# The first two units' output projection in seven products of halves, from combined weight blocks held in SBUF

## The chip, the cores and the metric

The kernel runs on one core of one Trainium2 chip. The metric is the device time of one execution in microseconds; a kernel's time is the median of its runs.

## What is computed

A retention block is followed by a gated feed-forward block. The inputs q, k and v have 8 batches, 8 heads, 576 positions and 64 channels. Cut to what matters:

```python
scores = (q @ k.transpose(0, 1, 3, 2)) / 8
Dmat = where(rel >= 0, gamma ** rel, 0)        # rel = pos[:, None] - pos[None, :], one gamma per head
attn = (scores * Dmat) @ v
x = attn.transpose(0, 2, 1, 3).reshape(4608, 512)
xn = x / sqrt(mean(x * x, axis=-1) + 1e-06) * rms_g
g = xn @ w_gate                                # 512 -> 1536
h = g / (1 + exp(-g)) * (xn @ w_val)
out = h @ w_out                                # 1536 -> 512
```

Activations are float32. The three weight matrices come in as 64-bit floats and are turned to float32 on the chip.

## The kernel before, in words

**Tiling.** The 4608 tokens are 12 units of 384. A unit's x is held transposed (`x_of`, 128 x 4 x 384: channels on partitions), and so is its hidden h (`h_of`, 128 x 12 x 384: hidden channels on partitions, 12 tiles of 128). The attention is done in 32 jobs, one for each batch and pair of heads. `slot(j)` (L397) computes the value products of job j-1, the scores and states of job j, weighs them on VectorE, and ends with the carried products of job j-1, whose results VectorE scales into x. `values` (L344) ends with a tiny GpSimd memset (`tick`, L359), and the first carried product (L370) waits for it: this keeps the order of rows in the array. `prepare` (L246) turns a job's q and k on VectorE (L251), `load_qk` and `load_kv` bring the next ones in on the SyncE queue. `following(j)` does the turn of job j+1 and the load of job j+2; q and k have one raw buffer each, so the load waits for the turn.

**Seven products.** From unit 2 on, both feed-forward stages multiply 2x2 blocks with seven products of half size in place of eight, after Winograd. The weights' combined blocks are called A11, A12, S1, A22, S2, S3 and S4 (S1 = A21 + A22, S2 = S1 - A11, S3 = A11 - A21, S4 = A12 - S2). For the up projections GpSimd makes them in place (`combine(m)`, L811 to L819: 12 operations of 128x512 for w_gate, m = 0, and 12 for w_val, m = 1). For the output, `across(u)` (L623) takes the halves of h: the blocks B11, B12 (first six tiles, left and right half of the tokens), B21 and B22. VectorE makes T1 = B12 - B11 and T3 = B22 - B12, later B11 + T3 and B21 - B11 (L649). `across` is a generator: the first step makes T1 and T3, and each later one issues one product of 12 matmuls of 128x192 (L637) in the order x, z, w, y, x, z, w; VectorE then adds the parts (L646), transposes the result in blocks of 32 (L659), and SyncE stores it in eight transfers of 24 KB (L669) for each of four quarters of the output. Three output tiles rotate, so the transpose of a fourth waits for the first one's stores.

**Blocks of w_out.** The seven blocks of w_out are kept in DRAM (`w_blocks`, stored by `keep`, L597), and `fetch` (L615) brings them one by one to four slots, in the room of w_out itself.

**The first two units.** Units 0 and 1 are computed while the weights still come in and are rounded, with plain products: `up_plain` (L552), then `down(u, s)` (L575), 12 matmuls of 128x512 (L578) into one bank for each 128 tokens, a copy on ScalarE (L583), one store. Unit 1's h lies in the upper half of w_val's room (blocks 8 to 13), and the upper half of w_gate's room serves the rounding as scratch until the last weights are done. After unit 1's last up product the order is: the turn of job 8 and the load of job 9, three blocks of w_out stored as they are, combine(0) on GpSimd, the three down parts of unit 1 with the norm of unit 2 between (squares on ScalarE added up by VectorE, L438; a mean by TensorE, L450; a power on GpSimd, L456; diagonals on VectorE, L463; a product that spreads them, L474; scaling and block sums on VectorE, L476 and L487), combine(1), slot 8 without a job before it, the down parts of unit 0, slot 9. The other four blocks of w_out are made by `combine_out` (L600), 24 VectorE operations of 128x256 (L608), one after each step of unit 2's up products, and are stored and fetched after them.

**What sets the order.** The order on each engine is the program's (`manual_schedule`): an instruction that waits holds all behind it on its engine. PSUM has five rotating banks, temporaries six rotating tiles; DMAs wait in turn for one of eight semaphores, so that an issue can wait for the landing of the eighth before it.

The stage as it stands, from `start`:

```python
        for u in (1, 0):
            for s in range(NS):
                down(u, s)
                if u == 1:
                    (norm_0, norm_1, norm_2)[s](2)
                    if s == 1:
                        diagonals(2)
            if u:
                combine(1)
                slot(8, rest=False)
                following(8)
        slot(9)
        following(9)
```

Of the kernel before, what the change touches and what calls it, by code (L numbers as in the profile page):

```python
# [41 lines left out]
def kernel(  # L42
# [44 lines left out]
    def bank(name):  # L87
        return banks.tile([P, 512], F32, tag="b", name=name)
# [483 lines left out]
                    nc.scalar.activation(out=h, in_=ps[:, :U], func=AF.Silu)  # L572
                yield

    def down(u, s):  # L575
        ps = bank(f"out_{u}_{s}")
        for f in range(NF):
            nc.tensor.matmul(  # L578
                ps[:, :DM], lhsT=h_of[u][:, f, s * P : s * P + P], rhs=w_out[:, f],
                start=(f == 0), stop=(f == NF - 1),  # L580
            )
        o = outs.tile([P, DM], F32, tag="o", name=f"o_{u}_{s}")
        nc.scalar.copy(out=o, in_=ps[:, :DM])  # L583
        nc.sync.dma_start(out=out[u * U + s * P : u * U + s * P + P, :], in_=o)


    ORDER = (A11, S1, S3, S2, A12, S4, A22)
    DH = DM // 2
    w_blocks = dram.tile([7, P, NH, DH], F32, name="w_blocks")
    w_slots = w_out.rearrange("p f d -> p (f d)").rearrange("p (s f d) -> p s f d", s=4, d=DH)  # L590
    n_fetched = 0

    def quarter(row, col):

        return w_out[:, col * NH : col * NH + NH, row * DH : row * DH + DH]

    def keep(blk, t):  # L597
        nc.sync.dma_start(out=w_blocks[blk], in_=t)

    def combine_out():  # L600

        a11, a12, a21, a22 = (quarter(r, c) for r in range(2) for c in range(2))
        for c in range(NH):
            for o, a, b, op in (
                (a22, a21, a22, ALU.add), (a21, a11, a21, ALU.subtract),
                (a11, a22, a11, ALU.subtract), (a12, a12, a11, ALU.subtract),
            ):
                nc.vector.tensor_tensor(out=o[:, c], in0=a[:, c], in1=b[:, c], op=op)  # L608
                yield
        for blk, t in ((S1, a22), (S3, a21), (S2, a11), (S4, a12)):  # L610
            keep(blk, t)
        for _ in range(4):
            fetch()

    def fetch():  # L615
        nonlocal n_fetched
        if n_fetched < 7 * (NU - 2):
            nc.sync.dma_start(
                out=w_slots[:, n_fetched % 4], in_=w_blocks[ORDER[n_fetched % 7]]
            )  # L620
            n_fetched += 1

    def across(u):  # L623


        h = h_of[u]
        b11, b12 = h[:, :NH, :HU], h[:, :NH, HU:]
        b21, b22 = h[:, NH:, :HU], h[:, NH:, HU:]
        t1 = ffn.tile([P, NH, HU], F32, tag="t1", name=f"t1_{u}")
        x_, y, z, w = (bank(f"{n}o_{u}") for n in "xyzw")  # L630
        s1, u2, u4 = (temp(f"{n}o_{u}") for n in ("m1", "u2", "u4"))

        def product(rhs, ps, start):
            k = 7 * (u - 2) + n_done
            for i in range(2):
                for c in range(NH):
                    nc.tensor.matmul(  # L637
                        ps[:, i * HU : i * HU + HU],
                        lhsT=w_slots[:, k % 4, c, i * P : i * P + P], rhs=rhs[:, c],
                        start=(start and i == c == 0), stop=False, skip_group_check=True,  # L640
                    )
            if n_done < 3:
                fetch()

        def add(o, a, ps):
            nc.vector.tensor_tensor(out=o, in0=a, in1=ps[:, :U], op=ALU.add)  # L646

        def block(o, a, b, op):
            nc.vector.tensor_tensor(out=o, in0=a, in1=b, op=op)  # L649

        def result(row, col, a, ps):
            r = ps[:, :U]
            if a is not None:
                r = temp(f"c{row}{col}_{u}")
                add(r, a, ps)
            o = outs.tile([P, DM], F32, tag="o", name=f"o_{u}_{row}_{col}")[:, :U]
            end = u == NU - 1
            if not end:
                nc.vector.transpose(out=o, in_=r)  # L659
            o_of = o.rearrange("p (d t r) -> p d t r", d=2, r=SQ)  # L660
            for d in range(2):
                if end:
                    half = slice(d * HU, d * HU + HU)
                    nc.vector.transpose(out=o[:, half], in_=r[:, half])
                for i in range(P // SQ):
                    c0 = row * DH + d * P + i * SQ
                    t0 = u * U + col * HU
                    queue = nc.scalar if end and i % 2 else nc.sync
                    queue.dma_start(  # L669
                        out=out[t0 : t0 + HU, c0 : c0 + SQ].rearrange("(t c) r -> c t r", c=SQ),  # L670
                        in_=o_of[i * SQ : i * SQ + SQ, d],
                    )

        n_done = 0
        block(t1, b12, b11, ALU.subtract)
        block(b12, b22, b12, ALU.subtract)
        yield
        product(b11, x_, True)
        nc.scalar.copy(out=s1, in_=x_[:, :U])
        block(b11, b12, b11, ALU.add)  # L680
        n_done += 1
        yield
        product(t1, z, True)
        n_done += 1
        yield
        product(b12, w, True)
        n_done += 1
        yield
        product(b11, y, True)
        add(u2, s1, y)  # L690
        add(u4, u2, z)
        result(1, 1, u4, w)
        n_done += 1
        yield
        product(b21, x_, False)
        result(0, 0, None, x_)
        block(b21, b21, b11, ALU.subtract)
        n_done += 1
        yield
        product(b22, z, False)  # L700
        result(0, 1, u2, z)
        n_done += 1
        yield
        product(b21, w, False)
        result(1, 0, u2, w)
        yield
# [147 lines left out]
    def start():  # L854
# [54 lines left out]
        gather(*squares.pop())  # L909
        load_qk(2 * NHP)  # L910
        load_kv(2 * NHP)
        for m, g in [(m, g) for g in range(NG) for m in range(2)]:
            for u in range(2):
                weights_to(4 * g + 2 * m + 1)
                for i, _ in enumerate(up_plain(u, m, g)):
                    if not (u or m or g):
                        if i == 0:
                            values(2 * NHP - 1)
                            carried(2 * NHP - 1)
                            gather(1, NHP - 1, square(1, NHP - 1))  # L920
                        elif i == 1:
                            norm_1(1)
                        elif i == 2:
                            diagonals(1)
                        elif i == 3:
                            norm_2(1)
                    weights(2)
                    act(1)
                    if i == 1:
                        weights_to(4 * g + 2 * m + 2)  # L930
        following(2 * NHP - 1)
        weights_to(len(chunks))
        for blk, row, col in ((A11, 0, 0), (A12, 0, 1), (A22, 1, 1)):
            keep(blk, quarter(row, col))
        combine(0)
        for u in (1, 0):
            for s in range(NS):
                down(u, s)
                if u == 1:
                    (norm_0, norm_1, norm_2)[s](2)  # L940
                    if s == 1:
                        diagonals(2)
            if u:
                combine(1)
                slot(8, rest=False)
                following(8)
        slot(9)
        following(9)

# [19 lines left out]
    with tc.manual_schedule():  # L969
        start()  # L970
        for u in range(2, NU):
            made = combine_out() if u == 2 else iter(())
            for i in range(2 * NG):
                for n, _ in enumerate(up(u, i % 2, i // 2)):
                    next(made, None)
                    if n == 2 and turns:
                        prepare_next(turns.pop())
                if u > 2 and i in (1, 3):
                    fetch()
                    fetch()  # L980
                if i == 2 * NG - 1:
                    rest = across(u)
                    next(rest)
                behind(u, i)
            for i, _ in enumerate(rest):
                if i == 0 and turns:
                    prepare_next(turns.pop())
                if i == 2:
                    behind(u, 6)
                    at, n = SLOTS[u % 3]  # L990
                    if 2 * NG - 1 in at:
                        load_next(u // 3 * 8 + n + len(at) - 1)
                elif i == 4:
                    behind(u, 7)
# [27 lines left out]
```

## Time and profile before

| what | value |
|---|---|
| median of three runs (lowest, highest) | 1153.94 us (1153.77, 1154.94) |
| the profiled execution's own time | 1159.48 us |
| its span in the profile | 1157.7 us |
| mean granted TensorE clock in it | 0.993 |
| busy in the span: TensorE, VectorE, ScalarE, GpSimd | 1133.4, 696.3, 246.1, 46.5 us |
| down products of unit 1, of unit 0 (L578) | 193.4 to 225.1, 226.9 to 258.0 us |
| combine(0), combine(1) on GpSimd (L819) | 184.07 to 200.76, 215.79 to 232.07 us |
| 24 operations of combine_out on VectorE (L608) | 416 ns each |
| a half-block subtraction of across (L649, 128x1152) | 1342 ns mean |
| store of one w_out block (768 KB), issue to landing | 6.0 us median |

Each row of the timeline has a start in microseconds from the span's start, a length, the engine, the line, the operation, the tiles written and read, the shape and the number of instructions merged; in brackets stands the engine's idle time before it, and who ended it. PE is TensorE, DVE VectorE, ACT ScalarE, POOL GpSimd, SP the SyncE queue. A float32 matmul shows as two records. The ends of matmuls are modelled, so the distance of starts tells their pace better than their lengths do.

### The profile page before, as it was taken

The numbers are of one execution on the slowest core, as the hardware profiler recorded it, in microseconds if no ns is written. First come the engines' busy times: TensorE is split into PE (matmuls) and PEld (weight loads), VectorE is DVE, ScalarE is ACT, GpSimd is POOL, SyncE is SP. The second block draws the span as 40 slices with busy tenths as digits, with TensorE's granted clock in tenths as the row PEclk, the third lists the DMA queues.
The fourth block names the chain that finished last, engine by engine and source line by source line (L and its number), as shares of the span: only waits on it lengthen the run. The fifth ranks groups of instructions, "written<-read, shape, count | busy, mean of one in ns | idle before, by whom it ended". The sixth has DMA issues, their size and how long they took to land.

```text
span 1157.7 us, 24337 instructions
## 1 busy us (share of the span) xinstructions
PE 1133.4 (98%) x10332; PEld 1024.5 (88%) x10332; DVE 696.3 (60%) x1414; ACT 246.1 (21%) x484; POOL 46.5 (4%) x74
## 2 busy tenths in 40 slices
PE   8789999999999999999999999999999999999998
PEld 6655555449999999999999999999999999999998
DVE  5778874328676585465775776465576576445352
ACT  5535641111211221111220220120220210120210
POOL 0000005500000000000000000000000000000000
PEclk8989999999999999999999999999999999999999
DMA  8855322322972556125335456306336413303304
GB/s 204 230 121 165 126 73 67 119 67 41 266 156 44 152 139 119 65 87 118 96 96 95 104 129 140 117 16 131 98 99 140 120 41 93 127 1 97 122 1 110
DMA packets 282412, 125.37 MB, mean 108 GB/s; under 512 B 257216, under 2 KB 264896, under 8 KB 282304
## 3 DMA queue, kind: packets, MB, share of 16 engines
q1 hardware_dynamic: 272160, 107.66, 37.4%
q10 hardware_dynamic: 10144, 16.16, 4.3%
q8 instruction: 81, 1.33, 0.5%
q14 instruction: 27, 0.22, 0.1%
HBM read 108.83 MB, written 14.94 MB: 107 GB/s over the span
## 4 chain that ended last, share of the span: by engine, by line
PE 93%; SPq 2%; DVE 2%; ACT 1%; issue 1%; DMA 1%; DVEq 0%; POOL 0%; POOLq 0%
PE w L507 13%; PE x L507 13%; PE z L507 13%; PE up L564 11%; PE xo L637 7%; PE wo L637 7%; PE zo L637 7%; PE y L507 7%; PE out L578 5%; PE yo L637 3%; PE av L351 2%; PE s L280 1%; PE av L370 1%; PE s L300 1%; SPq L161 1%
## 5 line engine op out<-in xcount | busy, mean ns | idle before, releaser
L531 ACT COPY m<-x 128x384 f32<-128x384 f32 x60 | 28.7, 478 | 430.7 <-PE x L507 406.7
L507 PE MATMUL w<-sums,w_val 128*128 128x192 f32 x480 | 88.6, 328 | 0.3
L507 PE MATMUL w<-sums,w_gate 128*128 128x192 f32 x480 | 88.0, 326 | 0.9 <-DVE h L514 0.8
L507 PE MATMUL z<-x,w_gate 128*128 128x192 f32 x480 | 87.9, 326 | 1.0 <-DVE u L514 1.0
L507 PE MATMUL x<-x,w_val 128*128 128x192 f32 x480 | 88.7, 328 | 0.0
L507 PE MATMUL x<-x,w_gate 128*128 128x192 f32 x480 | 88.5, 328 | 0.0
L507 PE MATMUL z<-x,w_val 128*128 128x192 f32 x480 | 87.8, 326 | 0.0
L637 PE MATMUL xo<-h,w_out 128*128 128x192 f32 x480 | 82.1, 328 | 0.0
L507 PEld LDWEIGHTS w<-sums,w_val 128*128 128x128 f32 x480 | 79.2, 190 | 2.7 <-DVE c L514 2.7
L637 PE MATMUL wo<-h,w_out 128*128 128x192 f32 x480 | 81.3, 326 | 0.0
L507 PEld LDWEIGHTS w<-sums,w_gate 128*128 128x128 f32 x480 | 79.4, 190 | 1.5 <-DVE h L514 1.5
L507 PEld LDWEIGHTS z<-x,w_gate 128*128 128x128 f32 x480 | 79.6, 190 | 1.3 <-DVE u L514 1.3
L514 DVE TENSOR_TENSOR u<-m,y 128x384 f32<-128x384 f32 x60 | 33.1, 552 | 77.5 <-PE y L507 77.5
L507 PEld LDWEIGHTS x<-x,w_val 128*128 128x128 f32 x480 | 79.2, 190 | 0.6
L507 PEld LDWEIGHTS x<-x,w_gate 128*128 128x128 f32 x480 | 79.3, 190 | 0.5
L507 PEld LDWEIGHTS z<-x,w_val 128*128 128x128 f32 x480 | 79.7, 190 | 0.0
L637 PEld LDWEIGHTS xo<-h,w_out 128*128 128x128 f32 x480 | 78.1, 190 | 0.5
L637 PEld LDWEIGHTS wo<-h,w_out 128*128 128x128 f32 x480 | 78.5, 190 | 0.0
L514 DVE TENSOR_TENSOR h<-u,w 128x384 f32<-128x384 f32 x60 | 33.1, 551 | 69.2 <-PE w L507 69.2
L564 PE MATMUL up<-x,w_gate 128*128 128x384 f32 x192 | 65.7, 502 | 0.9 <-DVE x L476 0.7
L526 ACT ACTIVATE h<-h 128x384 f32<-128x384 f32 x90 | 47.0, 523 | 91.3 <-DVE h L514 91.2
L564 PE MATMUL up<-x,w_val 128*128 128x384 f32 x192 | 62.6, 487 | 0.0
(155 smaller groups left out, 1747.0 us busy)
## 6 DMA issues: line engine op xcount, KB each, us to landing
w_out<-w_blocks SPq DMA_DIRECT2D x70, 768.0 KB, 4.9
out_dram<-o SPq DMA_DIRECT2D x304, 24.0 KB, 1.6
qraw<-in_q_dram SPq DMA_DIRECT2D x96, 72.0 KB, 2.7
kraw<-in_k_dram SPq DMA_DIRECT2D x96, 72.0 KB, 3.4
k<-in_k_dram SPq DMA_DIRECT2D x48, 128.0 KB, 3.0
v<-in_v_dram SPq DMA_DIRECT2D x48, 128.0 KB, 2.9
w_blocks<-w_out SPq DMA_DIRECT2D x7, 768.0 KB, 6.0
w_out<-in_moe_w_gate_dram ACTq DMA_DIRECT2D x5, 1024.0 KB, 5.7
```

Source lines behind the costliest of these rows:

```text
L161: nc.sync.dma_start(out=t[:, :, e], in_=src[b, 2 * hp + e, : NFULL * P].rearrange("(c p) d -> p c d", p=P),)
L280: nc.tensor.matmul(s[side(odd), e, i * L : i * L + L], lhsT=d["kT"][side(e), c * L : c * L + L], rhs=d["qT"][side(e), c * L : c * L + L], ...
L300: nc.tensor.matmul(o[side(e)], lhsT=d["k"][side(odd), i, e], rhs=d["v"][side(odd), i, e], start=True, stop=True,)
L351: mm = nc.tensor.matmul(av[odd][column(j, odd, e), i * L : i * L + L], lhsT=d["v"][side(odd), i, e] if c < NC - 1 else d["vt"][:, e], rhs= ...
L370: mm = nc.tensor.matmul(av[odd][column(j, odd, e), i * L : i * L + L], lhsT=d["sum"][side(e), c - 1], rhs=d["qT"][side(e), c * L : c * L + L],
L507: nc.tensor.matmul(ps[:, i * HU : i * HU + HU], lhsT=w_up[m][:, 2 * blk + c, cut], rhs=t_of[u][blk][:, c], start=(start and i == c == 0), ...
L514: nc.vector.tensor_tensor(out=o, in0=a, in1=pairs_of(ps), op=ALU.add)
L526: nc.scalar.activation(out=o, in_=c, func=AF.Silu)
L531: nc.scalar.copy(out=s1, in_=pairs_of(x_))
L564: nc.tensor.matmul(ps[:, :U], lhsT=w_up[m][:, 4 * half + c, i * P : i * P + P], rhs=x_of[u][:, c], start=(c == 0), stop=(c == NHP - 1),)
L578: nc.tensor.matmul(ps[:, :DM], lhsT=h_of[u][:, f, s * P : s * P + P], rhs=w_out[:, f], start=(f == 0), stop=(f == NF - 1),)
L637: nc.tensor.matmul(ps[:, i * HU : i * HU + HU], lhsT=w_slots[:, k % 4, c, i * P : i * P + P], rhs=rhs[:, c], start=(start and i == c == 0) ...
```

## The change

`down` is gone. The three combined blocks S1, S3 and S2 of w_out are made by four VectorE operations of 128x1536 into the upper half of w_gate's room, which the rounding has left by then, and S4 goes where A21 lay. They stand one after each of the last four steps of unit 1's up products. All seven blocks are then stored to DRAM from where they lie, on the SyncE queue, ahead of the load of job 9. Units 1 and 0 go through `across`, with the weights read from those places in SBUF (`first_blocks`) and no fetch. T1 and T3 of unit 1 are made ahead of the turn of job 8, those of unit 0 ahead of combine(1), slot 8 and the turn of job 9. The norm of unit 2 is placed between unit 0's products: the squares after the second, the mean after the third, the spreading product after the fifth. combine(0) follows unit 0's products, since the blocks lie in w_gate's room, and stands ahead of slot 9; combine(1) stands after unit 1's. Unit 2's `combine_out` steps are gone, and its first four fetches are issued two by two during its up products, as in later units.

```diff
--- before.py
+++ after.py
@@ -572,21 +572,11 @@
                     nc.scalar.activation(out=h, in_=ps[:, :U], func=AF.Silu)
                 yield
 
-    def down(u, s):
-        ps = bank(f"out_{u}_{s}")
-        for f in range(NF):
-            nc.tensor.matmul(
-                ps[:, :DM], lhsT=h_of[u][:, f, s * P : s * P + P], rhs=w_out[:, f],
-                start=(f == 0), stop=(f == NF - 1),
-            )
-        o = outs.tile([P, DM], F32, tag="o", name=f"o_{u}_{s}")
-        nc.scalar.copy(out=o, in_=ps[:, :DM])
-        nc.sync.dma_start(out=out[u * U + s * P : u * U + s * P + P, :], in_=o)
-
 
     ORDER = (A11, S1, S3, S2, A12, S4, A22)
     DH = DM // 2
     w_blocks = dram.tile([7, P, NH, DH], F32, name="w_blocks")
+    first_blocks = {}
     w_slots = w_out.rearrange("p f d -> p (f d)").rearrange("p (s f d) -> p s f d", s=4, d=DH)
     n_fetched = 0
 
@@ -599,18 +589,19 @@
 
     def combine_out():
 
+
         a11, a12, a21, a22 = (quarter(r, c) for r in range(2) for c in range(2))
-        for c in range(NH):
-            for o, a, b, op in (
-                (a22, a21, a22, ALU.add), (a21, a11, a21, ALU.subtract),
-                (a11, a22, a11, ALU.subtract), (a12, a12, a11, ALU.subtract),
-            ):
-                nc.vector.tensor_tensor(out=o[:, c], in0=a[:, c], in1=b[:, c], op=op)
-                yield
-        for blk, t in ((S1, a22), (S3, a21), (S2, a11), (S4, a12)):
-            keep(blk, t)
-        for _ in range(4):
-            fetch()
+        s1, s3, s2 = (
+            w_up[0][:, i : i + 2].rearrange("p b f -> p (b f)").rearrange("p (f d) -> p f d", d=DH)
+            for i in (8, 10, 12)
+        )
+        for o, a, b, op in (
+            (s1, a21, a22, ALU.add), (s3, a11, a21, ALU.subtract), (s2, s1, a11, ALU.subtract),
+            (a21, a12, s2, ALU.subtract),
+        ):
+            nc.vector.tensor_tensor(out=o, in0=a, in1=b, op=op)
+            yield
+        first_blocks.update({A11: a11, A12: a12, S1: s1, A22: a22, S2: s2, S3: s3, S4: a21})
 
     def fetch():
         nonlocal n_fetched
@@ -632,14 +623,15 @@
 
         def product(rhs, ps, start):
             k = 7 * (u - 2) + n_done
+            a = first_blocks[ORDER[n_done]] if u < 2 else w_slots[:, k % 4]
             for i in range(2):
                 for c in range(NH):
                     nc.tensor.matmul(
                         ps[:, i * HU : i * HU + HU],
-                        lhsT=w_slots[:, k % 4, c, i * P : i * P + P], rhs=rhs[:, c],
+                        lhsT=a[:, c, i * P : i * P + P], rhs=rhs[:, c],
                         start=(start and i == c == 0), stop=False, skip_group_check=True,
                     )
-            if n_done < 3:
+            if u > 1 and n_done < 3:
                 fetch()
 
         def add(o, a, ps):
@@ -909,6 +901,7 @@
         gather(*squares.pop())
         load_qk(2 * NHP)
         load_kv(2 * NHP)
+        made = combine_out()
         for m, g in [(m, g) for g in range(NG) for m in range(2)]:
             for u in range(2):
                 weights_to(4 * g + 2 * m + 1)
@@ -926,24 +919,31 @@
                             norm_2(1)
                     weights(2)
                     act(1)
+                    if u and m and g == NG - 1:
+                        weights_to(len(chunks))
+                        next(made, None)
                     if i == 1:
                         weights_to(4 * g + 2 * m + 2)
+        for _ in made:
+            pass
+        for blk, t in first_blocks.items():
+            keep(blk, t)
+        rest = across(1)
+        next(rest)
         following(2 * NHP - 1)
-        weights_to(len(chunks))
-        for blk, row, col in ((A11, 0, 0), (A12, 0, 1), (A22, 1, 1)):
-            keep(blk, quarter(row, col))
+        for _ in rest:
+            pass
+        rest = across(0)
+        next(rest)
+        combine(1)
+        slot(8, rest=False)
+        following(8)
+        for i, _ in enumerate(rest):
+            if i in (1, 2, 4):
+                (norm_0, norm_1, norm_2)[i // 2](2)
+                if i == 2:
+                    diagonals(2)
         combine(0)
-        for u in (1, 0):
-            for s in range(NS):
-                down(u, s)
-                if u == 1:
-                    (norm_0, norm_1, norm_2)[s](2)
-                    if s == 1:
-                        diagonals(2)
-            if u:
-                combine(1)
-                slot(8, rest=False)
-                following(8)
         slot(9)
         following(9)
 
@@ -969,13 +969,11 @@
     with tc.manual_schedule():
         start()
         for u in range(2, NU):
-            made = combine_out() if u == 2 else iter(())
             for i in range(2 * NG):
                 for n, _ in enumerate(up(u, i % 2, i // 2)):
-                    next(made, None)
                     if n == 2 and turns:
                         prepare_next(turns.pop())
-                if u > 2 and i in (1, 3):
+                if i in (1, 3):
                     fetch()
                     fetch()
                 if i == 2 * NG - 1:
```

## The prediction

> **What bounds the kernel now.** I read the page's busy shares first, then the chain of waits around the stage that the diff touches, then TensorE's timeline there, then VectorE's and GpSimd's timelines over the same microseconds.
>
> ```profile
> span 1157.7 us, 24337 instructions
> PE 1133.4 (98%) x10332; PEld 1024.5 (88%) x10332; DVE 696.3 (60%) x1414; ACT 246.1 (21%) x484; POOL 46.5 (4%) x74
> PE 93%; SPq 2%; DVE 2%; ACT 1%; issue 1%; DMA 1%; DVEq 0%; POOL 0%; POOLq 0%
> ```
>
> TensorE holds 93% of the chain: less matmul work is less time, unless another engine comes last in that stage. The chain (start, microseconds, what), over 180 to 460 us:
>
> ```profile
> 193.51 20.60 PE out L578 x48
> 214.68 10.41 PE out L578 x24
> 226.94 31.10 PE out L578 x72
> ...
> 325.07 4.10 PE xo L637 x24
> 329.16 3.90 PE zo L637 x24
> ```
>
> Down projections of units 1 and 0 cost 31.0 and 31.1 us; a product of halves costs 3.90 (24 records, two for each of 12 matmuls). TensorE's timeline of unit 2 shows its only idle time nearby (in brackets):
>
> ```profile
> 268.11 1.57 PE L507 MATMUL z<-x,w_gate 128*128 128x192 f32 x8 [0.96 <-DVE u L514]
> 291.17 1.57 PE L507 MATMUL w<-sums,w_gate 128*128 128x192 f32 x8 [0.85 <-DVE h L514]
> ```
>
> There VectorE is late: attention turns with the small L608 operations between them. Last, GpSimd and VectorE side by side:
>
> ```profile
> 215.79 16.28 POOL L819 TENSOR_TENSOR w_val<-w_val 128x512 f32<-128x512 f32 x12
> 215.85 2.69 DVE L463 TENSOR_SCALAR diag<-ident,r 128x128 f32<-128x128 f32 x3 [0.97 <-POOL r L456]
> 225.77 2.19 DVE L476 SCALAR_TENSOR_TENSOR x<-x,rms_g,rb 128x384 f32<-128x384 f32 x4 [7.23 <-PE rb L474]
> 227.99 1.40 DVE L487 TENSOR_TENSOR sums<-x 128x384 f32<-128x384 f32 x1
> 229.43 1.51 DVE L487 TENSOR_TENSOR x<-x 128x384 f32<-128x384 f32 x1
> 230.97 1.51 DVE L487 TENSOR_TENSOR sums<-x 128x384 f32<-128x384 f32 x1
> 232.51 0.56 DVE L487 TENSOR_TENSOR sums<-x,sums 128x384 f32<-128x384 f32 x1
> ```
>
> Until 232.07, while GpSimd combines, the L487 subtractions take 1.5 us each; the next, after it, 0.56. The L463 diagonals take 2.69 for three against 0.68 elsewhere (338.70 to 339.38). L476, with one operand in PSUM, isn't slowed.
>
> **What the Trainium skill says.** "SBUF — State Buffer", section Who interferes with whom: a VectorE instruction with two SBUF inputs contends with a GpSimd instruction that reads SBUF, the loser waiting for the whole of the other; with at most one SBUF input, outside the two-port modes, it doesn't. The trace agrees on all counts. "VectorE: DVE Perf Modes", the perf-mode tier table: fp32 tensor_tensor runs at 1x. The trace agrees: 0.56 us for 384 elements, 1.35 for 1152 (L649), so 1.03 ns an element. "Perfetto Trace Analysis", Identifying the Most-Contended Engine: matmul busy time misleads, being pipelined; so I sum start-to-start pitches.
>
> **The change, part by part.** Times are on the trace's axis, then from E1, the end of unit 1's seventh product.
>
> (1) TensorE. Before, from the first down matmul (193.35) to unit 2's first product (260.39) are 67.04 us. After, unstalled: seven products 27.6 (unit 2's take 28.81 from 325.07 to 353.88, with 1.21 of ms and rb between), slot 8 1.14, seven with ms and rb 28.81, slot 9 2.42: together 60.0. Gain 7.07.
>
> (2) Combining w_out. 24 operations of 0.42 leave unit 2; four of 128x1536 enter between unit 1's last multiplications, each 1.35 + 384 x 1.03 ns = 1.74. VectorE's ledger: the last weights done at 185.6 (1.22 for L805, no longer 2.05: GpSimd is idle then), multiplications to 187.5, then S1, multiplication, S3, multiplication, S2, last multiplication at 194.1, S4 195.8, T1 197.2, T3 198.5, turns of job 8 200.0. TensorE wants T1 at 197.45 and T3 at 201.3: 0, at most 0.5 if VectorE is later by half a microsecond. T1 hides behind product x alone.
>
> (3) Unit 2 without the L608 operations. At slot 10, four of them (1.5 us) lie ahead of the h that TensorE awaits; the 0.85 goes. At slot 9, 0.64 of them lie ahead of u: counted in (4).
>
> (4) The place where it goes back. combine(1) on GpSimd can start when unit 1's last product has read half its rows, E1 - 1.6, E1 being 193.35 + 27.6 = 220.95. It and combine(0) then keep GpSimd busy to about E1 + 37, and VectorE's two-input operations of that time contend: T1, T3 and B11 of unit 0, three additions of squares, three diagonals, B21, four L487. Before, most of this wasn't there or ran with GpSimd idle. That T1 and T3 stand ahead in the program doesn't help: the engines run at once. A two-input operation arriving at a busy GpSimd waits up to 1.27, then takes its own 1.35 or 0.56; back to back with GpSimd the small ones come every 1.54. From E1: c10 and its transpose to 1.2; T1 to 3.6, T3 to 5.95; weighing 0.9, sums 2.75 with the gap, turns of job 9 1.45, to 11.0; B11 to 12.25; three squares at 1.54 to 16.9. TensorE, unstalled, arrives at ms at 1.15 + 3 x 3.9 = 12.9: it waits 4.0 us. Behind ms are queued all products from y on. Next ms 0.76 and r 0.16 to 17.9, GpSimd's twelfth operation about 18.1, its power 0.87 to 19.0, diagonals 2.7 to 21.75; y ends 21.5, so u2, u4, c11 and its transpose run to 24.1; x's second half ends 25.4, its transpose 26.05; B21 to 27.9; L476 2.1 to 30.0; L487 4 x 1.54 to 36.1; c01, c10 and transposes 2.3 to 38.4; weighing of slot 9 and x 2.7 to 41.1; sums 2.5, turns 1.45, u and u4 1.1: 46.2. The bank for unit 2's sixth product comes free there, at 267.15 against 268.11 before. Gain 0.95 of a possible 7.07 + 0.64.
>
> (5) The memset behind which carried(8) waits is queued on GpSimd behind combine(0): 19.0 + 12 x 1.34 + 1.8 for contention, about 37; TensorE arrives at 35.7. It waits 1.3, inside VectorE's 46.2: nothing more, as VectorE is later anyway.
>
> (6) SP. Seven blocks are stored (0.65 us an issue) ahead of job 9's loads; those, 13 issues of 0.5 us, also wait for the turns at 199.3; then 32 stores of 24 KB a unit in place of three of 256 KB. Four stores of blocks started at 297.9 and the fetch waiting for them went out at 306.75: 2.2 us each, so seven are down by about 202 and unit 1's first output stores by 217.5. The transpose at E1 + 0.6 = 221.5 needs these: hidden, by 4 us. The fetches of unit 2 move ahead of their old place: nothing. ScalarE loses six copies of 0.585 and gains two: off the path.
>
> Sum: (4) 0.95 + (3) 0.85 = 1.8 us. The profiled execution took 1159.48 (span 1157.7), 0.5% above the median of the runs, 1153.94; a saving of microseconds carries over. **1152.1.**
>
> The unknown in (4) is when each operation meets GpSimd. From below: no waits, rival A. From above: B11 and B21 waiting fully (+1.9), T1 half a microsecond late: 1154.6. I take the phases of the ledger, which follow from the seen pattern.
>
> **Rivals.**
> A. Contention doesn't reach the path: without waits VectorE has the squares at about 11.6, before TensorE's 12.9. Then 7.07, 0.64 of the wait at slot 9 and 0.85 are gained, 8.56 in all: 1145.4. For: VectorE is only 60% busy. Against: fourteen two-input operations lie inside GpSimd's window, and the trace shows the price.
> B. Slower: the stores of blocks are the last to finish. The page's median landing is 6.0 us for one; if seven follow one another so, from 186 on, the last is down at 228. Job 9's last kraw load waits for that one, and 13 further issues (6.5 us) and 1.6 of landing put unit 1's first output at 236.1, E1 + 15.15. The transpose at E1 + 0.6 waits for it, T1 stands behind it on VectorE and product z on T1. GpSimd being through by then, T1 to squares take 11.1, to 26.9; diagonals at 31.5 instead of 21.75: 9.8 later, 1161.9. It decides from 3.9 us a block on. Against: 2.2 seen with four in flight. For: seven are more, and their sources in w_out are short rows.
>
> **How the numbers follow.** Forecast 0.68 (its own range 1149.5 to 1154.9), A 0.20, B 0.12. Leaving B out, the range is 1145.2 to 1155.2. A measurement tells about 0.2%, 2.3 us, from no change: faster takes A and 0.28 of the forecast's 0.68 (below 1151.6), slower takes B: 0.48, 0.40, 0.12.
>
> **What would show it.** Right: a wait at ms of 2 to 5 us ended by VectorE's squares; the half-block subtractions (L641 in the changed kernel) of unit 0 above 2 us and L438 near 1.5; products of 3.90 otherwise; TensorE not idle before unit 1's z; no wait of h at slot 10. Wrong: squares done before TensorE comes (A), an output transpose waiting for stores (B), or TensorE idle in the first seven products.

## The result and the profile after

The changed kernel takes 1154.68 us (median of four runs, 1153.73 to 1156.72); the kernel before, run beside it, 1154.02 (1153.77 to 1154.94). The ratio is 1.0007, interval [0.9989, 1.0024]: no difference that this measurement can tell. The forecast of 1152.1, 0.9984 of the time before, lies just below that interval; the time lies inside the range, near its upper end. So the size expected was not reached, and a saving of 7 us in TensorE's work left no trace in the time. The profiled execution took 1156.72 (span 1154.9).

The page after, first the span, then busy times, the instruction queue's row (packets, megabytes) and the chain by engine:

```profile
span 1154.9 us, 24803 instructions
PE 1128.6 (98%) x10524; PEld 1056.0 (91%) x10524; DVE 719.0 (62%) x1420; ACT 243.7 (21%) x480; POOL 51.0 (4%) x74
q8 instruction: 83, 1.36, 0.5%
PE 92%; DVE 4%; issue 1%; ACT 1%; DMA 1%; SPq 0%; DVEq 0%; POOL 0%; ACTq 0%; POOLq 0%
```

VectorE's share of the chain went from 2% to 4%: it holds the end in a place where it did not before. That place is found by cutting the program at three points of TensorE's timeline and taking differences of starts: the first matmul after the up products of units 0 and 1, unit 2's first product, and unit 2's first output product (xo).

| profiled execution | up products end | to unit 2's first product | to its xo | xo to the end |
|---|---|---|---|---|
| before | 193.35 | 67.04 | 131.65 | 832.7 |
| after | 190.86 | 64.94 | 130.81 | 833.3 |

Everything before 190 us is the same matmul work, and its end moves by several microseconds between executions that are alike up to there (186.69 to 190.86 in those of the change and of experiments 1, 2, 3 and 8 below); the stage itself, 131.65 against 130.81, is what the change touches. It gained 0.8, and 0.6 of that went again later. TensorE's timeline in the stage, in part:

```profile
227.37 4.06 PE L629 MATMUL wo<-h,w_gate 128*128 128x192 f32 x24
234.16 0.80 PE L450 MATMUL ms<-mean_w,sq 128*128 128x1 f32 x6 [2.73 <-DVE sq L438]
234.82 5.83 PE L629 MATMUL yo<-h,w_gate 128*128 128x192 f32 x24
240.48 4.06 PE L629 MATMUL xo<-h,w_out 128*128 128x192 f32 x24
...
255.17 0.69 PE L370 MATMUL av<-qT,sum 64*64 64x64 f32 x32 [0.40 <-POOL tick L359]
...
263.62 1.57 PE L507 MATMUL z<-x,w_gate 128*128 128x192 f32 x8 [1.06 <-DVE u L514]
...
275.52 0.69 PE L351 MATMUL av<-ret,v 64*64 64x64 f32 x32
...
278.98 0.38 PE L370 MATMUL av<-qT,sum 64*64 64x64 f32 x9 [1.26 <-issue]
279.30 1.57 PE L507 MATMUL x<-x,w_gate 128*128 128x192 f32 x8
```

Four things are to be seen. The wait at ms is there, ended by the squares (2.73 idle). The product after it starts at 234.82 and the next at 240.48: 5.66, where a product behind ms takes 3.98 (experiment 3 below) and others 3.90. Unit 2's z still waits for VectorE's u. And at slot 10 TensorE stops for 1.26 inside the carried products with "issue", which names no engine; slot 11 has another of 0.75. Slot 10 takes 3.78 (275.52 to 279.30) where it took 2.25 before, slot 11 3.33 for 2.24. The wait of h at slot 10 (0.85) is gone.

The granted clock around the slow product (columns: window, length, busy time and instructions of PE, PEld, DVE, ACT, POOL, then PEclk, DMA share, GB/s):

```profile
234.00:235.00 1.00, 0.84 (x7) 0.87 (x8) 0.02 (x2) 0.00 (x0) 1.00 (x1) 1.00 1.03 234
235.00:236.00 1.00, 1.00 (x4) 1.00 (x4) 0.16 (x1) 0.51 (x1) 0.92 (x2) 0.52 0.32 71
236.00:237.00 1.00, 1.00 (x4) 1.00 (x4) 0.00 (x0) 0.82 (x3) 1.00 (x2) 0.50 0.00 0
237.00:238.00 1.00, 1.00 (x5) 1.00 (x5) 0.67 (x1) 0.17 (x1) 1.00 (x2) 0.50 0.00 0
238.00:239.00 1.00, 1.00 (x6) 1.00 (x5) 1.00 (x3) 0.00 (x0) 0.92 (x2) 0.78 0.00 0
239.00:240.00 1.00, 1.00 (x9) 1.00 (x8) 1.00 (x1) 0.00 (x0) 0.94 (x1) 1.00 0.00 0
```

From 235 to 238.5 TensorE runs at half its clock. VectorE and GpSimd over the same time, lines picked from both timelines:

```profile
216.78 19.70 POOL L811 TENSOR_TENSOR w_val<-w_val 128x512 f32<-128x512 f32 x12 [144.93 <-PE wo L629]
219.45 1.31 DVE L641 TENSOR_TENSOR t<-h 128x1152 f32<-128x1152 f32 x1
220.80 2.31 DVE L641 TENSOR_TENSOR h<-h 128x1152 f32<-128x1152 f32 x1
227.60 1.80 DVE L641 TENSOR_TENSOR h<-h 128x1152 f32<-128x1152 f32 x1
229.32 4.69 DVE L438 TENSOR_TENSOR sq<-sq,sq 128x384 f32<-128x384 f32 x3
237.27 17.82 POOL L811 TENSOR_TENSOR w_gate<-w_gate 128x512 f32<-128x512 f32 x12
237.33 2.69 DVE L463 TENSOR_SCALAR diag<-ident,r 128x128 f32<-128x128 f32 x3 [2.18 <-POOL r L456]
249.36 1.50 DVE L487 TENSOR_TENSOR x<-x 128x384 f32<-128x384 f32 x1
250.90 1.51 DVE L487 TENSOR_TENSOR sums<-x 128x384 f32<-128x384 f32 x1
```

T3 takes 2.31 beside GpSimd for 1.36 without it (experiment 1), the squares 1.56 each for 0.63, the diagonals 2.69 for 0.68: the contention that the forecast priced. Not every operation met it: T1 took 1.31.

### The profile page after: what moved, and what is told of

It is laid out like the page before. It is cut to its first block, busy times and chain, and to the rows that moved or that the text cites. A ratio compares the mean times of both kernels' runs of the same rounds, so it can differ in the third digit from the quotient of the medians.

```text
span 1154.9 us, 24803 instructions
## 1 busy us (share of the span) xinstructions
PE 1128.6 (98%) x10524; PEld 1056.0 (91%) x10524; DVE 719.0 (62%) x1420; ACT 243.7 (21%) x480; POOL 51.0 (4%) x74
## 3 DMA queue, kind: packets, MB, share of 16 engines
q8 instruction: 83, 1.36, 0.5%
## 4 chain that ended last, share of the span: by engine, by line
PE 92%; DVE 4%; issue 1%; ACT 1%; DMA 1%; SPq 0%; DVEq 0%; POOL 0%; ACTq 0%; POOLq 0%
PE w L507 13%; PE x L507 13%; PE z L507 13%; PE up L564 11%; PE xo L629 8%; PE wo L629 7%; PE zo L629 7%; PE y L507 7%; PE yo L629 4%; PE av L351 2%; PE av L370 2%; PE s L280 1%; PE s L300 1%; PE rb L474 1%; PE ms L450 1%
## 5 line engine op out<-in xcount | busy, mean ns | idle before, releaser
L629 PE MATMUL xo<-h,w_out 128*128 128x192 f32 x528 | 90.3, 328 | 0.0
L629 PEld LDWEIGHTS xo<-h,w_out 128*128 128x128 f32 x528 | 85.9, 190 | 0.6
L629 PE MATMUL wo<-h,w_out 128*128 128x192 f32 x504 | 85.3, 326 | 0.0
L629 PEld LDWEIGHTS wo<-h,w_out 128*128 128x128 f32 x504 | 82.5, 190 | 0.0
L564 PE MATMUL up<-x,w_gate 128*128 128x384 f32 x192 | 63.3, 488 | 0.9 <-DVE x L476 0.7
```

The lines of the kernel that those rows point to most:

```text
L564: nc.tensor.matmul(ps[:, :U], lhsT=w_up[m][:, 4 * half + c, i * P : i * P + P], rhs=x_of[u][:, c], start=(c == 0), stop=(c == NHP - 1),)
L629: nc.tensor.matmul(ps[:, i * HU : i * HU + HU], lhsT=a[:, c, i * P : i * P + P], rhs=rhs[:, c], start=(start and i == c == 0), stop=False, ...
```

## The experiments

Three theories stood after the profile. **C**: VectorE's contention with GpSimd's combinations sets the waits. **K**: a long wait of TensorE costs again, by the slow clock after it. **R**: the "issue" pauses come from refills of TensorE's instructions. Rivals: the pauses come from other DMA traffic; the rest of the change (blocks, stores, L608) pays or costs, not the products. Each kernel was timed beside the kernel before. A table of all stages stands at the end of this part.

**1. No combinations.** combine(0) and combine(1) are left out, so the up products of unit 2 and later use plain blocks where combined ones belong.

```diff
         next(rest)
-        combine(1)
         slot(8, rest=False)
...
-        combine(0)
         slot(9)
```

> The changed kernel without GpSimd's 24 combining operations (the combined weights of the up projections are left out, so units 2 to 11 multiply with what lies in their place). Contention theory: T1, T3, B11 and B21 of unit 0 take 1.35 us each, the additions of squares 0.56, the block sums 0.56; no wait at the mean and none for the memset; unit 2's sixth product comes at about 39 us after unit 1's end in place of 45.5; the pauses in slots 10 and 11 stay; about 6 us under the changed kernel, ratio to before about 0.9945. Rival (VectorE is late by its amount of work): TensorE still waits over 1 us at the mean, and less than 3 us are gained.

1146.66 us, ratio 0.9936 [0.9920, 0.9952]. VectorE's timeline:

```profile
218.15 1.36 DVE L641 TENSOR_TENSOR h<-h 128x1152 f32<-128x1152 f32 x1
225.23 1.88 DVE L438 TENSOR_TENSOR sq<-sq,sq 128x384 f32<-128x384 f32 x3
230.56 0.68 DVE L463 TENSOR_SCALAR diag<-ident,r 128x128 f32<-128x128 f32 x3 [1.03 <-POOL r L456]
```

The same operations at their own length, and TensorE does not wait at ms or at slot 9's memset; unit 2's first product comes at 59.66, the seven products' full gain (67.04 before). C holds. A pause of 1.17 at slot 11 stays.

**2. Norm of unit 2 between unit 1's products,** where GpSimd is idle.

```diff
+        for i, _ in enumerate(rest):
+            if i in (1, 2, 4):
+                (norm_0, norm_1, norm_2)[i // 2](2)
+                if i == 2:
+                    diagonals(2)
         rest = across(0)
```

> The changed kernel with the norm of unit 2 moved from unit 0's products to unit 1's, where VectorE has 8 us idle and GpSimd is idle. Contention theory: TensorE's wait of 2.7 us at the mean goes; combine(0) then starts about 2.4 us earlier but TensorE comes 6 us earlier, so the wait for the memset behind it grows from 0.4 to about 3.4 us; unit 2's sixth product comes about 3.9 us earlier after unit 1's end than in the changed kernel (41.6 in place of 45.5 us); the pauses in slots 10 and 11 stay. Time about 3.9 us under the changed kernel, ratio to before about 0.9965. Rival (VectorE's amount of work, not GpSimd, makes it late, or the norm's place is of no account): no wait for the memset, less than 1.5 us gained.

1152.56 us, ratio 0.9981 [0.9974, 0.9988]: half of what was expected. The wait at ms is gone, but with nothing before it TensorE now comes earlier to the carried products of slot 9, which need GpSimd's memset, queued behind combine(0):

```profile
252.48 1.13 PE L370 MATMUL av<-qT,sum 64*64 64x64 f32 x32 [4.03 <-POOL tick L359]
253.54 2.93 PE L507 MATMUL x<-x,w_gate 128*128 128x192 f32 x8
256.26 2.27 PE L507 MATMUL y<-sums,w_gate 128*128 128x192 f32 x8
258.37 1.46 PE L507 MATMUL z<-x,w_gate 128*128 128x192 f32 x8
```

After 4.03 idle, the carried products take 1.13 for 0.69 and products x and y 2.72 and 2.11 from start to start for 1.40 and 1.30. The wait has changed its place, and K's price came with it.

**3. 32 tiny matmuls ahead of unit 2's ms.** They add 64 records, so that together with the change's 192 the count of matmul records ahead of unit 2 is 256 more than before. 10524 records (and as many weight loads) and 83 packets of 16 KB on queue q8 are 127 records to a packet: 256 are two packets, and the refills fall again where they fell before.

```diff
         ms = bank(f"ms_{u}")
+        if u == 2:
+            for i in range(32):
+                e = side(i % 2)
+                nc.tensor.matmul(ms[e, 64:128], lhsT=ones[e, :L], rhs=ones[e, :L], start=True, stop=True)
```

> The changed kernel with 32 tiny matmuls (64x64, results unused) put ahead of unit 2's mean products, where TensorE waits 2.7 us for VectorE anyway, so they should cost nothing. They bring the count of TensorE's instructions ahead of slot 10 back to a whole number of 16 KB refills from what the kernel before had there. Theory (the stage gains what the ledger said, and refills of TensorE's instructions that now fall into slots 10 and 11 give it back): the pauses of 1.26 us in slot 10 and 0.75 us in slot 11 go, and the time is some 2.0 to 2.6 us under the changed kernel, ratio to before about 0.998. Rival (the pauses come from the moved transfers, or are chance): they stay, ratio about 1.0007.

1150.47 us, ratio 0.9971 [0.9960, 0.9982]. TensorE's timeline:

```profile
227.19 2.08 PE L452 MATMUL ms<-ones 64*64 64x64 f32 x64
229.90 0.83 PE L456 MATMUL ms<-mean_w,sq 128*128 128x1 f32 x6 [0.63 <-DVE sq L438]
230.59 4.15 PE L635 MATMUL yo<-h,w_gate 128*128 128x192 f32 x24
234.57 4.06 PE L635 MATMUL xo<-h,w_out 128*128 128x192 f32 x24
...
251.00 1.13 PE L370 MATMUL av<-qT,sum 64*64 64x64 f32 x32 [2.14 <-POOL tick L359]
252.06 2.73 PE L513 MATMUL x<-x,w_gate 128*128 128x192 f32 x8
```

No pause is left in slots 10 and 11, as R says. And the product after ms takes 3.98 (230.59 to 234.57), not 5.66, although ms starts 2.71 after the wait began: TensorE was busy for 2.08 of it. Then the memset is late (2.14) and the slow clock comes there.

**4. The same 32 in the kernel before.** The edit of experiment 3 made to the kernel before.

> The kernel before with the same 32 tiny matmuls ahead of unit 2's mean products, where TensorE is busy: they cost about 1.0 us themselves. Refill theory: they shift the refills of TensorE's instructions as the change did, so pauses of about 1.3 and 0.8 us (with the slower pace around them 2.6 in all) come up in slots 10 and 11: 3.0 to 3.6 us slower than before, ratio about 1.003. Rival: 1.0 us slower, ratio 1.0009, no pauses there.

1160.63 us, ratio 1.0055 [1.0039, 1.0070], more than expected. The stage takes 138.26, 6.6 more: 2.1 for the 32 themselves (nothing hides them there), 3.2 in slot 11, which now has a pause of 2.85 that the kernel before lacks, and 1.7 in the slow products after it (2.43 and 1.96 from start to start for 1.40 and 1.30), less 0.4 of smaller waits that went. Slot 10, where a pause was expected too, has none. A pause comes with the count of matmuls, then, without the change.

**5. 32 tiny matmuls at the very start,** in the changed kernel, beside the six that open the program.

> The change with 32 tiny matmuls (64x64) more at the very start and nothing else. Refill theory: the wait at ms (2.7) and the slow product after it (5.66 in place of 3.98) stay, the pauses inside the carried products of slots 10 and 11 go: the stage from the end of the up products to unit 2's first output product takes 128.2 in place of 130.8, ratio 0.998. Rival (other DMA traffic pauses TensorE): both pauses stay, 130.8, ratio 1.0007.

The stage went to 128.19, as R had it (128.2), with no pause in slots 10 and 11. TensorE around ms:

```profile
229.52 4.06 PE L629 MATMUL wo<-h,w_gate 128*128 128x192 f32 x24
236.30 0.80 PE L450 MATMUL ms<-mean_w,sq 128*128 128x1 f32 x6 [2.72 <-DVE sq L438]
236.96 5.83 PE L629 MATMUL yo<-h,w_gate 128*128 128x192 f32 x24
242.62 4.06 PE L629 MATMUL xo<-h,w_out 128*128 128x192 f32 x24
```

It has the same matmuls as experiment 3, in another place, and the slow product is back (5.66). That sets K apart from R: the slow clock goes with the idle time, the pauses with the count. The kernel's time, though, is 1158.03, ratio 1.0027 [1.0016, 1.0039], where 0.998 was expected. What is lost lies in the start, which the expectation left out: its attention slots are bursts of short matmuls too. In the profiled execution, which took 1155.82, the start has pauses of 2.68 and 2.43, and the up products end at 193.01.

**6. All but the seven products.** Plain down products for units 1 and 0, the blocks of w_out made early, S4 after the last down product, combine(0) ahead of slot 9, unit 2 without its L608 operations.

> The kernel before with everything of the change but the seven products: units 1 and 0 keep plain down products, the combined blocks of w_out are made in unit 1's last up steps, combine(0) stands ahead of slot 9, unit 2 loses the 24 L608 operations. My theory: the wait of h at slot 10 (0.85 us) and 0.64 of the wait at slot 9 go, the matmul count and so the position of the instruction refills stay as before: 1152.5 us, ratio 0.9987, no pause inside the carried products of slots 10 and 11. Rival (the moved combining costs at the start, on VectorE or by the seven stores): the down products of unit 1 start later or wait, ratio 1.000 to 1.002.

1161.38 us, ratio 1.0054 [1.0034, 1.0075]. This version made a wait of its own: combine(0)'s fourth operation overwrites what S4 is made from, so GpSimd stands until the last down product has read that block (S4 begins at 249.24), and the memset behind it.

```profile
228.39 4.46 POOL L825 TENSOR_TENSOR w_gate<-w_gate 128x512 f32<-128x512 f32 x3
251.13 11.77 POOL L825 TENSOR_TENSOR w_gate<-w_gate 128x512 f32<-128x512 f32 x9 [18.28 <-issue]
262.84 0.09 POOL L359 MEMSET tick<- 1x1 f32 x1
```

TensorE waited 6.76 at the memset. It says what a memset behind twelve operations can cost, and nothing of the products; so it was made again as follows.

**7. As 6, with slot 9's memset on VectorE.**

```diff
-        d["valued"] = nc.gpsimd.memset(tick, 0.0)
+        d["valued"] = (nc.vector if j == 2 * NHP else nc.gpsimd).memset(tick, 0.0)
```

> As the version with everything of the change but the seven products, with slot 9's memset on VectorE, so that it doesn't stand behind combine(0), which in that version waits for S4 and so for unit 0's last down product. My theory: the wait of 6.76 at the memset and the slow clock after it go; what is left of the change without its products is the wait of h at slot 10 (0.85) and 0.64 of that at slot 9: the stage 130.2 in place of 131.65, ratio 0.9987. Rival: unit 2's products wait for combine(0) themselves, which works through nine of its twelve operations only from 251 us on: 2 us or more of waits at z or w of unit 2, ratio 1.001 to 1.003.

1151.39 us, ratio 0.9984 [0.9976, 0.9993], stage 129.70: with the memset out of GpSimd's queue, the change without its products, in substance L608 taken out of unit 2, is worth 1.95. The whole change, with the products, has the longer stage (130.81).

**8. Norm early and the memset on VectorE:** the edits of 2 and 7 in the changed kernel.

> The change with the norm of unit 2 between unit 1's products, and the memset that slot 9's carried products wait for on VectorE in place of GpSimd, where it stood behind combine(0). My theory: neither the wait at ms (2.73) nor that at the memset (4.03 in the version with the norm early) is left, nor the slow clock that follows such waits; one pause at slot 11 stays, as the matmul count is the same. From the end of the up products to unit 2's first output product 122.2 (the version without GpSimd's combinations less its two idle times) + 1.2 to 1.5 = 123.6 against 131.65 before: ratio 0.993. Rival: the wait moves once more (unit 2's product y on combine(0), or z on VectorE's turn of job 10) by 2 us or more, with the slow clock after it: ratio 0.996 to 0.998.

1149.13 us, ratio 0.9942 [0.9920, 0.9963]. Unit 2's first product is at 59.66, as without any combinations, though GpSimd runs both in full: T3 is still slowed (2.31), but TensorE has no wait at ms or at the memset; of the waits for VectorE 0.63 at z is left. Pauses of 0.34 and 1.29 at slots 10 and 11 are left (stage 124.69, 1.1 above what was expected).

**9. As 8, with 32 tiny matmuls at the very start.**

> As the version with norm early and the memset on VectorE, with 32 tiny matmuls (64x64) more beside the six at the very start, where TensorE waits for its first data anyway. Refill theory (the pauses in slots 10 and 11 come from where the instruction refills, one for 64 matmuls, fall in a burst of 70 short matmuls): the pause at slot 11 goes, 122.2 to 122.6 for the stage, ratio 0.992; the start may change by a microsecond or two, since its slots are such bursts too. Rival (the pauses come from other DMA traffic at that time): the pause stays, ratio as without the 32.

The stage is 122.46, no pause. The time is 1152.43, ratio 0.9975 [0.9964, 0.9987], as the start grew: in its profile two pauses of 3.5 and 3.4, and the up products end at 196.24.

**10. As 8, with the 32 behind the start's slots,** ahead of unit 1's first up product, where TensorE waits 0.7 for x.

```diff
                 ps = bank(f"up_{u}_{m}_{half}_{i}")
+                if u == 1 and not (m or g or half or i):
+                    for n in range(32):
+                        e, at = side(n % 2), U + n // 2 % 8 * 16
+                        nc.tensor.matmul(ps[e, at : at + 16], lhsT=ones[e, :L], rhs=ones[e, :16], start=True, stop=True)
```

> The change with the norm early, slot 9's memset on VectorE, and 32 tiny matmuls (64x64, 16 columns) ahead of unit 1's first up product, where TensorE waits 0.7 us for x in every run: behind the attention slots of the start, so that these stay as they are. Refill theory: the up products end at most 1 us later than without them, the pauses of slots 10 and 11 (0.34 and 1.29) are gone and the stage from the end of the up products to unit 2's first output product takes 122.5 in place of 124.7: ratio 0.993. Rival (the start's slots were lengthened in the version with 32 more at the very start for another reason than the position of the refills, or the pauses come from other traffic): the stage stays at 124.7 or the start grows by 4 us or more, ratio 0.995 to 0.998.

1145.18 us, ratio 0.9926 [0.9912, 0.9939], the fastest of all. The stage, 122.46, explains 2.2 of the 4.0 us that it is under experiment 8; the rest lies outside it. All of TensorE's waits from 190 to 330 us in its profile, against those of the changed kernel ("issue" names no engine):

```profile
PE z L507 <- DVE u L514: 0.6, 1, 0.6
```

```profile
PE ms L450 <- DVE sq L438: 2.7, 1, 2.7
PE av L370 <- issue: 2.0, 2, 1.3
PE z L507 <- DVE u L514: 1.1, 1, 1.1
PE av L370 <- POOL tick L359: 0.4, 1, 0.4
```

Each ratio is to the kernel before run in the same set, whose median was 1153.75 to 1154.61. In every profile the stretch from xo to the end takes 832.5 to 833.6.

| kernel | to unit 2's first product | to its xo | us, median | ratio |
|---|---|---|---|---|
| before | 67.04 | 131.65 | 1154.02 | |
| the change | 64.94 | 130.81 | 1154.68 | 1.0007 |
| 1 no combinations | 59.66 | 123.90 | 1146.66 | 0.9936 |
| 2 norm early | 64.35 | 129.94 | 1152.56 | 0.9981 |
| 3 32 at ms | 65.37 | 128.47 | 1150.47 | 0.9971 |
| 4 32 at ms, in before | 69.10 | 138.26 | 1160.63 | 1.0055 |
| 5 32 at the start | 64.94 | 128.19 | 1158.03 | 1.0027 |
| 6 all but the products | 74.38 | 138.32 | 1161.38 | 1.0054 |
| 7 as 6, memset moved | 66.95 | 129.70 | 1151.39 | 0.9984 |
| 8 norm early, memset moved | 59.66 | 124.69 | 1149.13 | 0.9942 |
| 9 as 8, 32 at the start | 59.66 | 122.46 | 1152.43 | 0.9975 |
| 10 as 8, 32 later | 59.66 | 122.46 | 1145.18 | 0.9926 |

Take the stage and that stretch from the median, and 188.8 to 191.9 are left for the start (with the 1.8 between span and time) in ten of the kernels, 197.0 and 197.4 in the two with the 32 at the very start (5 and 9): an estimate, as each kernel has one profile.

What a refill does, from the trace's records of the instruction queue's 16 KB packets. A slot lasts 2.25 without a pause.

| kernel, slot | slot starts | packet starts | first matmul after the pause | packet to matmul |
|---|---|---|---|---|
| after, 10 | 275.52 | 276.71 | 278.98 | 2.27 |
| after, 11 | 297.69 | 298.51 | 300.76 | 2.25 |
| 8, slot 10 | 269.49 | 269.77 | 272.03 | 2.26 |
| 8, slot 11 | 290.74 | 292.09 | 294.35 | 2.26 |
| 4, slot 11 | 298.95 | 301.67 | 304.12 | 2.45 |
| before, 10 | 280.01 | 281.72 | none | |
| 3, slot 10 | 271.63 | 273.44 | none | |
| 10, slot 10 | 267.29 | 268.99 | none | |

The change and experiments 1, 2, 4 and 8 have a pause in slot 10 or 11; the other seven kernels have none there. Where a pause falls is told by counting TensorE's matmul records from the first. In all twelve traces, up to 330 us, every pause over 0.3 us that names no engine ends with record 348, 476, 602 or 603, 729, 981 or 983, 1108, 1235, 2508, 2636, 2763 or 2764. These lie whole packets of 126 to 128 records apart, whatever matmul stands there: in 5 and 9, whose 64 tiny records come first, record 603 is a matmul of L300, where record 602 of the others is one of L230. The last packet before such a record began 2.20 to 2.96 us ahead of it.

The reading is that TensorE pauses where a new packet's matmuls come up sooner than that. A packet that starts early in a slot is not enough: in the change, the slots at 380.77 and 401.72 have one 0.51 and 1.12 after their start and no pause. Counted on in steps of 127, their first matmuls would stand at about 384 and 405, behind these slots. What decides when a packet starts is open: the change and experiment 1 give TensorE the same matmuls in the same order, and only the change pauses in slot 10. No run measured a packet by itself.

## Why the prediction was right or wrong

**(1) TensorE's work.** 60.0 was forecast, 59.66 is reached where nothing waits (experiments 1, 8, 9, 10): a gain of 7.4 for 7.07. Right.

**(2) Combining w_out.** Four operations of 1.74 to 1.75; T1 and T3 of unit 1 ready at 195.95, and TensorE goes through unit 1's products at 3.90 without idle time. Right.

**(3) L608.** The wait of h at slot 10 is gone; experiment 7 measures 1.95 for this part, 0.85 + 0.64 was said. Right in kind, 0.5 too small.

**(4) Contention.** The mechanism and the place are shown by experiment 1. Of the sizes, the wait at ms was 2.73 for 4.0: T1 met no operation of GpSimd's in its way (1.31, not 2.4), B11 took 1.80 for 1.25, and the squares ended 15.9 after E1 (218.15), not 16.9. Unit 2's sixth product came at E1 + 45.5 for 46.2. This looks like a good hit, but by errors that cancel. Product y began 0.9 earlier than forecast, took 5.66 where the term "y ends 21.5" gives it its usual 3.90, and so ended 0.8 late. VectorE's work from the next product's end on was then 1.6 shorter than in the ledger: B21 (1.34 for 1.85) and the first block sum (0.77 for 1.54) met no operation in their way. The wait at ms costs 4.6 in all: 2.89 itself, and 1.67 in the product behind it. In the signs to look for, "products of 3.90 otherwise" was wrong for the same reason.

That a wait can cost again could have been read before. The Trainium skill's page "TensorE: Matmul & The Clock Gate", Part 1, says that TensorE is held at half its clock by default, that activity releases it, and that it falls back after an idle window of about 3.4 us. The kernel before had a case of its own, a wait of 3.07 that ended at 60.98, with a clock of 0.50 from 59.95 to 66.78. The traces agree on the half, not on how long TensorE must be idle. Waits of 2.06 (at 36.6 us in experiment 10) and 2.14 (experiment 3) were followed by the half clock; 1.78 (at 37 us in experiment 7) was not, but neither were 2.60 (at 37.7 in the kernel before) and 2.33 (at 37.6 in experiment 3). So the length of a wait alone does not decide. Up to 330 us the twelve traces have 27 stretches of half clock, each 3.41 or 6.83 long, and within a trace they start whole multiples of 3.41 apart. Over the 3.41 just before, TensorE was busy for at most 0.46 of the time in 25 of them (0.63 and 0.74 in two); in the steps of 3.41 that held most of the waits of 2.60 and 2.33 it was busy for 0.51 and 0.54. How a wait falls across these steps seems to decide; no run moved one wait across them.

**(5) The memset.** It ran at E1 + 36.9, 37 was forecast; TensorE waited 0.40 there. "Nothing more, as VectorE is later anyway" holds for the change as it is, and hid that the memset is the next thing late: with the wait at ms out of the way it costs 4.03 (experiment 2).

**(6) SP and stores.** The last of the seven blocks is issued at 193.31, the first output store at 209.10, no transpose waits on the path. Right; rival B did not come about.

**The sum.** Forecast: 0.95 up to unit 2's sixth product and 0.85 after it. Measured from the end of the up products, the first is 2.00 (74.76 before, 72.76 after) and the second is turned into a loss of 1.2. From the unstalled stage, 122.46 with its one wait at z: + 2.89 for the wait at ms (6.79 from wo to ms, less 3.90) + 1.67 for the slow product + 0.64 at the memset + 0.41 more at z + 1.53 and 1.09 for slots 10 and 11 = 130.7, measured 130.81. The term that the forecast did not have is the last: **2.6 us for the instruction stream**, as the change's 96 matmuls more are an odd number of half packets (192 records, one packet and a half). It is the difference between a forecast gain of 1.8 and the 0.8 seen, and more than that: in experiment 5, where the pauses are gone and all else of the stage is as in the change, the stage gains 3.5. So it is luck that the stage's gain came out within 1 us of the forecast: what contention left is about twice what was forecast, and pauses that had no term took most of it back.

This too stood in the profile of before, as waits put down to "issue":

```profile
PE av L370 <- issue: 5.7, 2, 3.1
```

These are two pauses of 5.7 in all in the attention slots of its first 65 us, at records 729 and 1235. The skill's page "Runtime: NRT & Kernel Launch", Instruction fetch mechanics, says that instructions come in 16 KiB blocks and that crossing into the next is "mostly hidden". The trace agrees on the size (1.36 MB in 83 packets) and, while long products run, on the hiding; in bursts of short matmuls it costs up to 2.85 in the stage and 3.5 in the start (experiment 9).

**The rivals.** A, no contention, 1145.4: not this kernel, but its time is about right for experiment 1 (1146.66), and experiment 10 reaches it with the contention there, by other means. B is refuted.

What stays open: why the start differs by several microseconds between executions that are alike up to there, and so how much of any difference below 2 us is its own.

## What to carry to other kernels

When work moves beside work that is itself queued, list what the engine's queue holds behind it: here a memset of 90 ns behind twelve combinations kept TensorE idle for 4.03 us, and moving two small things (the norm, the memset) turned no gain into one of 0.6%, ratio 0.9942 [0.9920, 0.9963]. A wait of TensorE of 2 us or more can be followed by slow microseconds, here 1.2 to 2.1 more: price it with them, or keep TensorE busy through it. And when a change adds or removes matmuls, look at the dense bursts of short ones behind it: "issue" in the list of waits shows where instructions came late, and a gain of a few microseconds can be paid there.

## What the runs showed of the hardware that was not expected

- After waits of 2.06 to 6.76 us TensorE's granted clock can fall to 0.50, during the wait or up to 1.6 us after it, for 3.41 or 6.83 us; waits of 2.33 and 2.60 were also seen with no fall. The product behind a 2.73 wait took 5.66 for 3.98, and 3.98 when short matmuls had filled 2.08 of the wait.
- TensorE's instructions come in packets of 16 KB, one for 127 matmul records and their weight loads. Where the matmuls of a new packet come up within 2.2 to 3.0 us of its start, in bursts of short matmuls, TensorE pauses, for 0.34 to 3.5 us. The pauses stand whole packets apart in the count of records (602, 729, 981, 1108, 1235 in the kernel before), and 32 tiny matmuls far ahead took them away or brought them.
- 32 matmuls of 64x64 with 64 or with 16 columns cost the same, 2.04 to 2.08.
